# A planned attention and FFN kernel: eight exponentials of block 1 moved into block 0, a column-tiled key projection and another rule for zero matmuls

## The chip, the core and the metric

The kernel runs on one core of a Trainium2 chip. The core has a matrix engine (TensorE, PE in the profile, with its weight loads as PEld), a vector engine (VectorE, DVE), a scalar engine (ScalarE, ACT) for functions such as exp and tanh, a general engine (GpSimd, POOL) and DMA queues, here issued by SyncE (SP). Each engine works through its own list of instructions in order and waits for others by semaphores. Matmuls write to PSUM; everything else lies in SBUF. The metric is the time of one execution on the device, in microseconds; a lower time is better.

## What is computed

One sequence of 2048 tokens of width 512; 32 query heads of width 16 share one key head and one value head; the FFN has width 1792.

```python
x = A_x                                   # 1 x 2048 x 512, bf16
xn = layernorm(x)
q = heads(xn @ wq); k = xn @ wk; v = xn @ wv       # q: 32 heads of 16
s = softmax(q @ k.T * 16 ** -0.5) @ v              # every head, the same k, v
s = join(s) @ wo
g = silu((silu(xn @ w_gate) * (xn @ w_up)) @ w_down)
out = x + s * g
```

## The kernel before

**A plan, then the code.** The kernel holds a small planner in Python (`_Sched`, L182 on). Each piece of work is an `_Op` with an engine, a duration, what it depends on and a function that emits the instructions. The planner runs through time once while the kernel is being built; the order that comes out is then emitted and pinned, engine by engine, with `chain`. On the chip only this order remains: the planner's durations decide who stands behind whom, and waits do the rest.

**Prologue** (`pro_x`, `pro_mm`, `pro_v`). The tokens come in four chunks of 512. For each: statistics, normalization (DVE), transposes by matmul (PE, L434), eviction into `xnT` (DVE, L440), the key projection `pmm` (PE, L443, four steps over the 512 inner elements, with the key weights repeated to all 128 columns in `wk_rep`), its eviction into two key buffers KT[0] and KT[1] (DVE, L447), which are zero in the rows of the other half of the heads, and the value projection (PE, L451). The first chunk also gets the first query tile.

**Attention.** 32 blocks: 16 pairs (a quarter of the tokens and 8 heads), two halves of 4 heads each. A block goes over 16 key tiles of 128 keys, each in two parts x = 0, 1 (2 heads each), so 32 tiles of 128 keys by 2 x 512 queries. Per tile: two score matmuls into one of three PSUM buffers (ring, L836; each uses 32 rows of the array), then the exponential. In ring buffers 0 and 1 this is ACT's work (L887), written to one of eight bf16 buffers `Pb`; in ring buffer 2 it is DVE's (L914, then L927, L930 and L932 for each two tiles). DVE joins once 26 tiles are issued (`D_START`) and the prologue has released its buffers (`d_gate`). When both parts of a key tile have their exponentials, four value matmuls of 32 columns (L719) accumulate into `o_ps`, the one accumulator of the running block. `act_block` gives the block from which ACT takes its next tile: the first one with tiles left. Of block 0, a tile can only be taken once its keys are there (`tile_ready`).

**Fill.** Query projections, the FFN (L470; gate, tanh on ACT at L630, up, down) and the output projection are matmuls in column form: `cmm` cuts the 128 columns of a weight tile into four matmuls of 32 columns each at the four column positions of the array. They are handed out by `pump` at a rate that spreads the FFN over the attention tiles. `g_down` writes the FFN result of 128 tokens into `g2_sb`, which the output stage reads; nothing is in `g2_sb` before.

**PE's choice.** `pe_pick` gives PE's next piece of work at the planner's time F: the next ACT score (time `ts`), the best ready other matmul (`tm`, ranked by `rank`), or a DVE score. If the earliest of them is still at least a matmul (and a mode switch) away, after 26 tiles are issued, and fewer than 7 (`ZN`) column groups were started in the last 3.4 us (`c_log`), a zero group is put in: four column matmuls with zero weights `zw` that add nothing into the open accumulator `o_ps`. In the prologue, `junk` matmuls (L1149) into an unused buffer play that part until DVE's first pair.

Of the kernel before, what the change touches and what calls it, by code (L numbers as in the profile page):

```python
# [33 lines left out]
PB_URG, AHEAD, LAZY, ZN = 6, 16, 8, 7  # L34
# [147 lines left out]
class _Sched:  # L182
# [5 lines left out]
    def __init__(self):  # L188
        self.free = {"PE": 0.0, "ACT": 0.0, "DVE": 0.0, "POOL": 0.0, "DMA": 0.0}
        self.ready = {e: [] for e in self.free}  # L190
        self.done = []
        self.seq = 0
        self.mode = None
        self.key = lambda o: o.prio
# [53 lines left out]
    def place(self, op, start):  # L248
        e = op.eng
        op.start = start  # L250
        if e == "PE":
            op.start += self.switch(op.mode)
            self.mode = op.mode
        op.end = op.start + op.dur
        if e != "DMA":
            self.free[e] = op.end
        self.done.append(op)
        for u in op.users:
            u.left -= 1
            if u.left == 0:  # L260
                self._arm(u)
# [7 lines left out]
def kernel(  # L269
# [13 lines left out]
    nc = tc.nc  # L283
# [75 lines left out]
    Pb = [sb([P, 1024], BF16, f"Pb{i}") for i in range(NPB)]  # L359
    Ub = [sb([P, 2048], U16, f"Ub{i}") for i in range(NU)]  # L360
# [188 lines left out]
    def pro_mm(deps, bk, w, t0, t1, pr):  # L549
        last = None  # L550
        for kc in range(KC):
            last = OP("PE", MMF * (t1 - t0) / 512, deps + [brel[bk], last],
                      lambda kc=kc: e_mm(bank[bk][:, 0:t1 - t0], w, t0, t1, [kc]), (pr, t0), "f", "pmm")
        return last

    def pro_v(c, deps, bk, pr):
        a = None
        for i in range(4):
            a = OP("PE", 0.26, deps + [brel[bk], a, wv_in], lambda i=i: e_vmm(c, i, bank[bk]), (pr, i), "f", "vmm")
        e = OP("DVE", 0.17, [a], lambda: e_vev(c, bank[bk]), (pr - 0.2,), name="vev")  # L560
        brel[bk] = e
        d = [e]
        vs = []
        for i in (-1, 0, 1):
            d = [OP("POOL", 0.33, d, lambda i=i: e_vbuild(c, i), (0,), name="vb")]
            vs.append(d[0])
        v_ready.append(vs)
# [23 lines left out]
    for c in range(1, NSC):  # L591
        evs = pro_x(c, 1.0 + 0.01 * c, ("2a", "2b"), "DVE")
        kp = pro_mm(evs, "m", wk_of, 512 * c, 512 * c + 512, 0.5 + 0.01 * c)
        ka = OP("DVE", 0.62, [kp], lambda c=c: e_kev(512 * c, 512 * c + 512, bank["m"], 0), (0.5, c), name="kev")
        kb = OP("DVE", 0.62, [kp, ka], lambda c=c: e_kev(512 * c, 512 * c + 512, bank["m"], 1), (1.02 + 0.01 * c, c),
                name="kev")
        brel["m"] = kb
        k_ready.append([[ka], [kb]])
        pro_v(c, evs, "2a", 0.7 + 0.01 * c)
# [159 lines left out]
    cur = {"ba": 0, "lastx": 1, "nA": 0, "exp": None, "pair": None, "np": 0, "issued": 0, "lastsc": None, "junk": 0}  # L759
# [4 lines left out]
    pair_blk, c_log = [], []  # L764
# [27 lines left out]
    def act_block():  # L792
        b = cur["ba"]
        while b < NBLK and rem(b, 0) + rem(b, 1) == 0:
            b += 1
        return b if b < NBLK else None

# [60 lines left out]
    def check_done(b):  # L858
        if nx[b][0] == NT and nx[b][1] == NT and not (cur["pair"] is not None and cur["pair"][0] == b):
            assert not unp[b][0] and not unp[b][1]  # L860
            kb_ready[b] = cur["lastsc"]
            finish_block(b)
# [13 lines left out]
    def act_sc(i, b, x, start):  # L876
        sc, t = place_sc(i, b, x, start, MMF)
        cur["lastx"] = x
        cur["ba"] = b
        k = cur["nA"]  # L880
        cur["nA"] += 1
        pi = k % NPB
        pb_rel.append(None)
        if k >= NPB:
            assert pb_rel[k - NPB] is not None
        ex = OP("ACT", 0.904, [sc, pb_rel[k - NPB] if k >= NPB else None, cur["exp"]],
                lambda: nc.scalar.activation(out=Pb[pi][:], in_=ring[i][:], func=ACT.Exp, scale=escale, bias=ebias),  # L887
# [3 lines left out]
        unp[b][x].append((ex, k, t))  # L891
        if unp[b][0] and unp[b][1]:
            half = b % 2
            mms, dps, ks = [], [], []
            for xx in range(2):
                e_, k_, t_ = unp[b][xx].pop(0)
                mms += mm_of(VA, lambda g, k_=k_: Pb[k_ % NPB][:, (g % 2) * 512:(g % 2 + 1) * 512], t_, half,
                             (2 * xx, 2 * xx + 1))
                dps += [e_, v_ready[t_ // 4][0]]
                ks.append(k_)  # L900
            pv = OP("PE", MMF, dps + [oev[b - 1]], pv_emit(b, mms), (1, b, min(ks)), "c", "pv")
            blk_pv[b].append(pv)
            for k_ in ks:
                pb_rel[k_] = pv
# [145 lines left out]

    def pe_pick():
# [3 lines left out]
        b = act_block()  # L1055
# [16 lines left out]
        if ready:  # L1072
# [6 lines left out]
            def rank(o):  # L1079
# [5 lines left out]
                if o.mode == "f":  # L1085
                    return (0.5, o.prio)
# [24 lines left out]
        if junk and T - F > 0.3:  # L1111
            return F, ("junk", None)
        zb = act_block()
        zb = NBLK - 1 if zb is None else zb
        if not junk and cur["issued"] >= D_START and T - F >= MMF + sd.switch("c") \
                and sum(1 for q in c_log[-ZN:] if q > F - 3.4) < ZN:
            for bb in (zb - 1, zb):
                if bb >= 0 and oev[bb].start is None and oev[bb - 1].start is not None \
                        and sd.avail(oev[bb - 1], "PE") <= F and blk_pv[bb] and blk_pv[bb][0].start is not None \
                        and oev[bb].left > 0 and any(o.start is None for o in blk_pv[bb]):  # L1120
                    return F, ("zero", bb)
        if ts is not None and ts <= T + 1e-9:
# [8 lines left out]
    def pe_do(start, what):  # L1131
        kind, arg = what
        if kind == "op":
            sd.run(start, arg)
            if arg.mode == "c":
                c_log.append(start)
            return
        if kind == "zero":
# [5 lines left out]
            c_log.append(start)  # L1144
# [14 lines left out]
        b = act_block()  # L1159
# [136 lines left out]
```

## Time and profile before

| | |
|---|---|
| median of 9 runs | 794.9 us (789.57 to 800.91) |
| the profiled execution | 797.36 us, span 795.5 us |
| mean granted TensorE clock in it | 0.966 |
| busy: PE, DVE, ACT, POOL | 739.8 (93%), 736.7 (93%), 758.5 (95%), 51.2 us (6%) |
| exponentials on ACT (L887) | 778, busy 740.4 us |
| first passes on DVE (L914) | 246, busy 299.4 us |
| score matmuls on PE (L836) | 2048, busy 323.0 us |

The three large engines are all busy for more than nine tenths of the span. A group's busy time counts overlapping stretches once, so it can be less than the count times the mean. The idle time before a group is how long its engine stood still just before it, with the instruction that ended the wait. The clock that TensorE is granted is given as a share of the full one; at 0.5 it runs at half speed.

The prologue in order of time: the first exponential starts at 12.55 us, the first pass of DVE at 48.09 us, the first zero group at 69.3 us.

### The profile page before, as it was taken

How to read it: one execution, taken by the hardware profiler on the slowest of the kernel's cores; microseconds unless marked ns; L12 is line 12 of the kernel's file. 1: busy time of each engine (PE TensorE's matmuls, PEld its weight loads, DVE VectorE, ACT ScalarE, POOL GpSimd, SP SyncE). 2: the span in 40 equal slices, each digit the busy share in tenths (PEclk: the TensorE clock that was granted, in tenths of full speed). 3: DMA queues.
4: the chain of work that ended last, by engine and by line, in shares of the span. 5: the costliest groups of instructions: out<-in, count | busy, mean ns of one | idle time of the engine just before them, and what ended most of it. 6: DMA issues, size and time to landing. Idle time of an engine off the chain costs nothing.

```text
span 795.5 us, 19520 instructions
## 1 busy us (share of the span) xinstructions
PE 739.8 (93%) x8095; PEld 224.0 (28%) x8098; DVE 736.7 (93%) x925; ACT 758.5 (95%) x864; POOL 51.2 (6%) x59
## 2 busy tenths in 40 slices
PE   7899999999999999999999999999999989999994
PEld 3422322222222222222222222222222222222221
DVE  7649999999999999999999999999999989999994
ACT  6679999999999999999999999999999989999993
POOL 2200000100002000000002000000001200000001
PEclk8759999999999999999999999999999989999997
DMA  9300000000000000000001000000000000000001
GB/s 328 111 2 1 13 12 9 15 2 22 2 24 28 18 7 2 23 1 23 3 10 34 9 22 2 23 2 10 15 2 22 29 22 2 2 22 2 24 1 31
DMA packets 19464, 18.50 MB, mean 23 GB/s; under 512 B 8552, under 2 KB 15464, under 8 KB 19368
## 3 DMA queue, kind: packets, MB, share of 16 engines
q1 hardware_dynamic: 17496, 16.37, 6.8%
q8 instruction: 65, 1.06, 0.6%
q10 hardware_dynamic: 1872, 0.82, 0.4%
q14 instruction: 31, 0.25, 0.1%
HBM read 12.62 MB, written 2.34 MB: 19 GB/s over the span
## 4 chain that ended last, share of the span: by engine, by line
PE 51%; ACT 24%; DVE 16%; issue 5%; SPq 1%; DMA 1%; DVEq 0%; ACTq 0%
PE ring L836 22%; ACT Pb L887 19%; PE m_ps L470 17%; PE o_ps L719 10%; DVE Ub L914 6%; ACT th L630 4%; DVE Wb L932 3%; DVE Eb L930 2%; DVE Wb L927 2%; ACT th L647 1%; SPq L746 1%; DVE oa L732 1%; PE ring L434 1%; DVE hT L636 1%; DMA dn<-oa 1%
## 5 line engine op out<-in xcount | busy, mean ns | idle before, releaser
L887 ACT ACTIVATE Pb<-ring 128x1024 bf16<-128x1024 f32 x778 | 740.4, 1221 | 16.8 <-PE ring L836 15.9
L836 PE MATMUL ring<-QB,KT 32*128 32x512 bf16 x2048 | 323.0, 388 | 35.1 <-ACT Pb L887 29.1
L914 DVE TENSOR_SCALAR Ub<-ring 128x1024 uint16<-128x1024 f32 x246 | 299.4, 1217 | 12.4 <-PE ring L836 8.1
L836 PEld LDWEIGHTS <-KT 32*128 32x128 bf16 x2048 | 110.5, 91 | 347.9 <-issue 344.9
L719 PE MATMUL o_ps<-Pb,VA 128*32 128x512 bf16 x1556 | 153.5, 394 | 0.6 <-ACT Pb L887 0.5
L932 DVE TENSOR_TENSOR Wb<-Wb,Ub 128x2048 f16<-128x2048 f16 x123 | 152.0, 1235 | 0.0
L930 DVE TENSOR_SCALAR Eb<-Ub 128x2048 uint16<-128x2048 uint16 x123 | 85.5, 697 | 0.0
L927 DVE TENSOR_SCALAR Wb<-Ub 128x2048 uint16<-128x2048 uint16 x123 | 84.6, 687 | 0.1
L470 PE MATMUL m_ps<-xnT,wg_sb 128*32 128x512 bf16 x896 | 75.5, 389 | 0.7 <-DVE hT L636 0.7
L470 PE MATMUL m_ps<-wd_sb,hT 128*32 128x512 bf16 x896 | 72.2, 384 | 0.2 <-DVE g_sb L649 0.2
L470 PE MATMUL m_ps<-xnT,wu_sb 128*32 128x512 bf16 x896 | 70.6, 388 | 0.2 <-DVE ab L632 0.2
L704 POOL TENSOR_TENSOR oT<-oa,rb 128x512 bf16<-128x512 f32 x15 | 22.1, 1471 | 618.7 <-DMA rb<-dscr 486.9
L719 PEld LDWEIGHTS <-VA 128*32 128x32 bf16 x1556 | 38.9, 94 | 57.8 <-issue 57.4
L719 PE MATMUL o_ps<-Eb,VD 128*32 128x512 f16 x492 | 49.0, 388 | 1.5 <-DVE oa L732 0.6
L719 PE MATMUL o_ps<-Wb,VD 128*32 128x512 f16 x492 | 48.6, 384 | 1.4 <-DVE Wb L932 1.2
L630 ACT ACTIVATE th<-m_ps 128x512 f32<-128x512 f32 x56 | 44.5, 795 | 0.0
L636 DVE TENSOR_TENSOR hT<-ab,m_ps 128x512 bf16<-128x512 f32 x56 | 38.2, 681 | 3.3 <-PE m_ps L470 3.1
L719 PEld LDWEIGHTS <-VD 128*32 128x32 f16 x984 | 28.4, 93 | 41.4 <-issue 40.6
L632 DVE SCALAR_TENSOR_TENSOR ab<-th,m_ps 128x512 f32<-128x512 f32 x56 | 38.2, 682 | 1.9 <-ACT th L630 1.7
L732 DVE COPY oa<-o_ps 128x512 f32<-128x512 f32 (+1 forms) x33 | 22.0, 670 | 6.3 <-PE o_ps L719 5.9
L470 PEld LDWEIGHTS <-wg_sb 128*32 128x32 bf16 x896 | 17.3, 95 | 25.2 <-issue 24.5
L470 PEld LDWEIGHTS <-wu_sb 128*32 128x32 bf16 x896 | 15.4, 95 | 26.4 <-issue 25.2
(102 smaller groups left out, 252.8 us busy)
## 6 DMA issues: line engine op xcount, KB each, us to landing
rb<-dscr SPq DMA_DIRECT2D x15, 256.0 KB
dn<-oa SPq DMA_DIRECT2D x120, 2.0 KB, 1.7
oa<-oa SPq DMA_DIRECT2D x60, 32.0 KB, 2.0
wg_sb<-in_B_w_gate_dram SPq DMA_DIRECT2D x1, 1792.0 KB, 12.5
wu_sb<-in_B_w_up_dram SPq DMA_DIRECT2D x1, 1792.0 KB
wd_sb<-in_B_w_down_dram SPq DMA_DIRECT2D x1, 1792.0 KB, 19.7
out_dram<-xn SPq DMA_DIRECT2D x14, 128.0 KB, 1.9
x_sb<-in_A_x_dram SPq DMA_DIRECT2D x3, 512.0 KB
```

Source lines behind the costliest of these rows:

```text
L470: return [nc.tensor.matmul(out=dst[GRP * j:GRP * j + GRP, :], lhsT=w[:, GRP * j:GRP * j + GRP], rhs=rhs, start=start, stop=stop, tile_posi ...
L630: t_ = OP("ACT", 0.477, [a], lambda: nc.scalar.activation(out=th[i][:], in_=m_ps[:], func=ACT.Tanh, scale=0.5), (0,), name="tanh")
L632: s_ = OP("DVE", 0.6, [t_, ab_rel[i]], lambda: nc.vector.scalar_tensor_tensor(out=ab[i][:], in0=th[i][:], scalar=1.0, in1=m_ps[:], op0=ALU ...
L636: h = OP("DVE", 0.6, [b], lambda: nc.vector.tensor_tensor(out=hT[:, f, :], in0=ab[i][:], in1=m_ps[:], op=ALU.mult), (1,), name="hmul")
L719: r.append(nc.tensor.matmul(out=o_ps[GRP * g:GRP * g + GRP, :], lhsT=lhs, rhs=rhs, start=(n == 0), stop=(n == pv_total[(b, g)] - 1), tile_ ...
L732: oev[b] = sd.new(_Op("DVE", 0.6, [], lambda: [nc.vector.tensor_copy(out=oat[:, a:z], in_=o_ps[:, a:z]) for a, z in cuts], (0.2,), name="o ...
L836: return lambda: [nc.tensor.matmul(out=ring[sl][:, u * 512:(u + 1) * 512], lhsT=KT[half][GRP * g:GRP * g + GRP, t * P:(t + 1) * P], rhs=QB ...
L887: lambda: nc.scalar.activation(out=Pb[pi][:], in_=ring[i][:], func=ACT.Exp, scale=escale, bias=ebias),
L914: lambda: nc.vector.tensor_scalar(out=Ub[ui][:, x * 1024:(x + 1) * 1024], in0=ring[2][:], scalar1=ubias, scalar2=UINF, op0=ALU.add, op1=AL ...
L927: o1 = OP("DVE", 0.6, [pa, pa0, w_rel[u - NE] if u >= NE else None], lambda: nc.vector.tensor_scalar(out=Wb[ei][:], in0=Ub[ui][:], scalar1 ...
L930: o2 = OP("DVE", 0.6, [pa, pa0, e_rel[u - NE] if u >= NE else None], lambda: nc.vector.tensor_scalar(out=Eb[ei][:], in0=Ub[ui][:], scalar1 ...
L932: o3 = OP("DVE", 1.135, [o1, o2], lambda: nc.vector.tensor_tensor(out=Wb[ei][:].bitcast(FP16), in0=Wb[ei][:].bitcast(FP16), in1=Ub[ui][:]. ...
```

## The change

There are three edits, and some bookkeeping.

1. `now_block` takes the place of `act_block` in `pe_pick` and `pe_do`. While block 0 runs, it may return block 1 for ACT's next tile: when block 0's next tile has no keys yet or gets them later than PE is free, and block 1's next tile is ready earlier. Up to 8 such tiles may be taken (`XB`, eight views of 128 x 1024 in `g2_sb`), and a begun pair of parts is completed first. Their exponentials stay in `XB` until block 1 is the running block, since their value matmuls wait for the eviction of block 0 (`oev[b - 1]`).
2. `pro_mm` gets a mode: for chunks 1 to 3 the key projection is emitted by `cmm` (four matmuls of 32 columns per step) instead of one matmul of 128 columns. `pmm` keeps its rank among the prologue's work.
3. Zero groups are decided by `activity(F)`: the sum of planned durations of the PE work started in the last 3.4 us, where a score counts 0.107 and transposes and V projections count nothing. Below 1.7 (`ACTMIN`) a gap is filled; below 1.5 (`ACTLOW`) the gap is measured up to the next ACT score even if a full-array matmul is ready. The condition on 26 issued tiles falls away, and zeros come before `junk`. `fin_b` lets a block that is still being filled take zeros without a value matmul outstanding.

The planned duration of a V projection step goes from 0.26 to 0.13.

```diff
--- before.py
+++ after.py
@@ -31,7 +31,7 @@
 NWARM, NJUNK = 13, 200
 D_START, D_LIM, D_LIM_END = 26, 12, 8
 F_ON, F_OFF = 26, 60
-PB_URG, AHEAD, LAZY, ZN = 6, 16, 8, 7
+PB_URG, AHEAD, LAZY, ACTMIN, ACTLOW = 6, 16, 8, 1.7, 1.5
 TOL, MERGE = 0.12, 0.1
 
 
@@ -255,6 +256,8 @@
         if e != "DMA":
             self.free[e] = op.end
         self.done.append(op)
+        if e == "PE":
+            self.pe_log.append(op)
         for u in op.users:
             u.left -= 1
             if u.left == 0:
@@ -357,6 +360,7 @@
     QB = [sb([P, 512], BF16, f"QB{i}") for i in range(2)]
     NPB, NU, NE = 8, 3, 2
     Pb = [sb([P, 1024], BF16, f"Pb{i}") for i in range(NPB)]
+    XB = [g2_sb[:, 2 * i:2 * i + 2, :].rearrange("p n d -> p (n d)") for i in range(NT // 2)]
     Ub = [sb([P, 2048], U16, f"Ub{i}") for i in range(NU)]
     Eb = [sb([P, 2048], U16, f"Eb{i}") for i in range(NE)]
     Wb = [sb([P, 2048], U16, f"Wb{i}") for i in range(NE)]
@@ -546,17 +550,20 @@
                     evs.append(ev)
         return evs
 
-    def pro_mm(deps, bk, w, t0, t1, pr):
+    def pro_mm(deps, bk, w, t0, t1, pr, mode="f"):
         last = None
         for kc in range(KC):
-            last = OP("PE", MMF * (t1 - t0) / 512, deps + [brel[bk], last],
-                      lambda kc=kc: e_mm(bank[bk][:, 0:t1 - t0], w, t0, t1, [kc]), (pr, t0), "f", "pmm")
+            def emit(kc=kc):
+                if mode == "c":
+                    return cmm(bank[bk][:, 0:t1 - t0], w(kc), xnT[:, kc, t0:t1], kc == 0, kc == KC - 1)
+                return e_mm(bank[bk][:, 0:t1 - t0], w, t0, t1, [kc])
+            last = OP("PE", MMF * (t1 - t0) / 512, deps + [brel[bk], last], emit, (pr, t0), mode, "pmm")
         return last
 
     def pro_v(c, deps, bk, pr):
         a = None
         for i in range(4):
-            a = OP("PE", 0.26, deps + [brel[bk], a, wv_in], lambda i=i: e_vmm(c, i, bank[bk]), (pr, i), "f", "vmm")
+            a = OP("PE", 0.13, deps + [brel[bk], a, wv_in], lambda i=i: e_vmm(c, i, bank[bk]), (pr, i), "f", "vmm")
         e = OP("DVE", 0.17, [a], lambda: e_vev(c, bank[bk]), (pr - 0.2,), name="vev")
         brel[bk] = e
         d = [e]
@@ -590,7 +597,7 @@
     k_ready.append([[ke0, ke1], [kf0, kf1]])
     for c in range(1, NSC):
         evs = pro_x(c, 1.0 + 0.01 * c, ("2a", "2b"), "DVE")
-        kp = pro_mm(evs, "m", wk_of, 512 * c, 512 * c + 512, 0.5 + 0.01 * c)
+        kp = pro_mm(evs, "m", wk_of, 512 * c, 512 * c + 512, 0.5 + 0.01 * c, "c")
         ka = OP("DVE", 0.62, [kp], lambda c=c: e_kev(512 * c, 512 * c + 512, bank["m"], 0), (0.5, c), name="kev")
         kb = OP("DVE", 0.62, [kp, ka], lambda c=c: e_kev(512 * c, 512 * c + 512, bank["m"], 1), (1.02 + 0.01 * c, c),
                 name="kev")
@@ -756,12 +763,12 @@
 
     nx = [[0, 0] for _ in range(NBLK)]
     unp = [[[], []] for _ in range(NBLK)]
-    cur = {"ba": 0, "lastx": 1, "nA": 0, "exp": None, "pair": None, "np": 0, "issued": 0, "lastsc": None, "junk": 0}
+    cur = {"ba": 0, "lastx": 1, "nA": 0, "exp": None, "pair": None, "np": 0, "issued": 0, "lastsc": None, "junk": 0, "nX": 0}
     slot = [None, None, None]
     pb_rel, w_rel, e_rel, wop_rel = [], [], [], []
     open_block(0)
 
-    pair_blk, c_log = [], []
+    pair_blk, fin_b = [], set()
 
     def dve_key(o):
         if o.name in ("dM", "dE", "dW") and pair_blk[o.prio[1]] < cur["ba"]:
@@ -794,6 +801,19 @@
         while b < NBLK and rem(b, 0) + rem(b, 1) == 0:
             b += 1
         return b if b < NBLK else None
+
+    def now_block():
+        b = act_block()
+        if b == 0 and rem(1, 0) + rem(1, 1):
+            r = [tile_ready(bb, act_x(bb)) for bb in (0, 1)]
+            F = sd.free["PE"] + 0.15
+            if unp[1][0] + unp[1][1] and len(unp[1][0]) != len(unp[1][1]) and r[1] is not None and cur["nX"] < len(XB):
+                return 1
+            if len(unp[0][0]) != len(unp[0][1]) and r[0] is not None:
+                return 0
+            if cur["nX"] < len(XB) - 1 and r[1] is not None and (r[0] is None or r[0] > F and r[1] < r[0]):
+                return 1
+        return b
 
     def act_x(b, want=None):
         if want is not None and rem(b, want) > 0 and len(unp[b][want]) < 2:
@@ -858,6 +878,7 @@
     def check_done(b):
         if nx[b][0] == NT and nx[b][1] == NT and not (cur["pair"] is not None and cur["pair"][0] == b):
             assert not unp[b][0] and not unp[b][1]
+            fin_b.add(b)
             kb_ready[b] = cur["lastsc"]
             finish_block(b)
 
@@ -876,32 +897,39 @@
     def act_sc(i, b, x, start):
         sc, t = place_sc(i, b, x, start, MMF)
         cur["lastx"] = x
-        cur["ba"] = b
-        k = cur["nA"]
-        cur["nA"] += 1
-        pi = k % NPB
-        pb_rel.append(None)
+        pre = b == 1 and cur["ba"] == 0 and act_block() == 0
+        if pre:
+            k = -1 - cur["nX"]
+            buf = XB[cur["nX"]]
+            cur["nX"] += 1
+        else:
+            cur["ba"] = b
+            k = cur["nA"]
+            cur["nA"] += 1
+            buf = Pb[k % NPB][:]
+            pb_rel.append(None)
         if k >= NPB:
             assert pb_rel[k - NPB] is not None
         ex = OP("ACT", 0.904, [sc, pb_rel[k - NPB] if k >= NPB else None, cur["exp"]],
-                lambda: nc.scalar.activation(out=Pb[pi][:], in_=ring[i][:], func=ACT.Exp, scale=escale, bias=ebias),
+                lambda: nc.scalar.activation(out=buf, in_=ring[i][:], func=ACT.Exp, scale=escale, bias=ebias),
                 (1,), name="exp")
         cur["exp"] = ex
         slot[i] = ex
-        unp[b][x].append((ex, k, t))
+        unp[b][x].append((ex, k, t, buf))
         if unp[b][0] and unp[b][1]:
             half = b % 2
             mms, dps, ks = [], [], []
             for xx in range(2):
-                e_, k_, t_ = unp[b][xx].pop(0)
-                mms += mm_of(VA, lambda g, k_=k_: Pb[k_ % NPB][:, (g % 2) * 512:(g % 2 + 1) * 512], t_, half,
+                e_, k_, t_, b_ = unp[b][xx].pop(0)
+                mms += mm_of(VA, lambda g, b_=b_: b_[:, (g % 2) * 512:(g % 2 + 1) * 512], t_, half,
                              (2 * xx, 2 * xx + 1))
                 dps += [e_, v_ready[t_ // 4][0]]
                 ks.append(k_)
             pv = OP("PE", MMF, dps + [oev[b - 1]], pv_emit(b, mms), (1, b, min(ks)), "c", "pv")
             blk_pv[b].append(pv)
             for k_ in ks:
-                pb_rel[k_] = pv
+                if k_ >= 0:
+                    pb_rel[k_] = pv
         check_done(b)
         return sc
 
@@ -1048,11 +1076,19 @@
             job["acc"] += w
             fn()
 
+    def activity(F):
+        a = 0.0
+        for o in reversed(sd.pe_log):
+            if o.start < F - 3.4:
+                break
+            a += 0.107 if o.name == "sc" else 0.0 if o.name in ("tr", "vmm") else o.dur
+        return a
+
     def pe_pick():
         F = sd.free["PE"]
         ready = sd.ready["PE"]
         ts = None
-        b = act_block()
+        b = now_block()
         rel = [i for i in (0, 1) if slot[i].start is not None]
         if b is not None and rel:
             i = min(rel, key=lambda i: sd.avail(slot[i], "PE"))
@@ -1082,7 +1118,7 @@
                     if fin or outst >= PB_URG:
                         return (0, o.prio)
                     return (1 if o.name == "dpv" else 3, o.prio)
-                if o.mode == "f":
+                if o.mode == "f" or o.name == "pmm":
                     return (0.5, o.prio)
                 if o.name == "part":
                     return (4, o.prio)
@@ -1108,17 +1144,18 @@
         if not cands:
             return (F, ("junk", None)) if junk else None
         T = min(cands)
-        if junk and T - F > 0.3:
-            return F, ("junk", None)
         zb = act_block()
         zb = NBLK - 1 if zb is None else zb
-        if not junk and cur["issued"] >= D_START and T - F >= MMF + sd.switch("c") \
-                and sum(1 for q in c_log[-ZN:] if q > F - 3.4) < ZN:
+        act_ = activity(F)
+        Tz = ts if act_ < ACTLOW and ts is not None and tm is not None and co.mode == "f" else T
+        if Tz - F >= MMF + sd.switch("c") and act_ < ACTMIN:
             for bb in (zb - 1, zb):
                 if bb >= 0 and oev[bb].start is None and oev[bb - 1].start is not None \
                         and sd.avail(oev[bb - 1], "PE") <= F and blk_pv[bb] and blk_pv[bb][0].start is not None \
-                        and oev[bb].left > 0 and any(o.start is None for o in blk_pv[bb]):
+                        and oev[bb].left > 0 and (bb not in fin_b or any(o.start is None for o in blk_pv[bb])):
                     return F, ("zero", bb)
+        if junk and T - F > 0.3:
+            return F, ("junk", None)
         if ts is not None and ts <= T + 1e-9:
             return ts, ("act", i)
         if tm is not None and tm <= T + 1e-9:
@@ -1132,8 +1169,6 @@
         kind, arg = what
         if kind == "op":
             sd.run(start, arg)
-            if arg.mode == "c":
-                c_log.append(start)
             return
         if kind == "zero":
             o = _Op("PE", MMF, [oev[arg - 1]], pv_emit(arg, [(zw[:], xnT[:, 0, 0:512], g) for g in range(4)]), (0,), "c",
@@ -1141,7 +1176,6 @@
             o.seq = sd.seq
             sd.seq += 1
             sd.place(o, start)
-            c_log.append(start)
             blk_pv[arg].append(o)
             return
         if kind == "junk":
@@ -1156,7 +1190,7 @@
             dve_sc(arg[0], arg[1], start, MMF)
             return
         i = arg
-        b = act_block()
+        b = now_block()
         dt = None
         if d_ok() and slot[2].start is not None and sd.avail(slot[2], "PE") <= start + MERGE:
             x = act_x(b)
```

In the order that results, ACT still has 778 exponentials and DVE 246 first passes. ACT's exponentials 9 to 16 are those of block 1; their sixteen value matmuls stand after ACT's 46th score. There are 25 zero groups instead of 34. Of these, 23 stand between ACT's 4th and its 28th score; before, the first stood after the 46th.

## The prediction

> **What bounds the kernel now.** I read four views, in this order: the slices of the span, the waits of ScalarE (ACT), a table of stretches, and the timeline of the first 66 us.
>
> The page first: slice by slice the granted TensorE clock, and the group that carries ACT.
>
> ```profile
> PEclk8759999999999999999999999999999989999997
> ...
> L887 ACT ACTIVATE Pb<-ring 128x1024 bf16<-128x1024 f32 x778 | 740.4, 1221 | 16.8 <-PE ring L836 15.9
> ```
>
> The clock is below full in the first 60 us (three slices), once near 650 us, and at the end. ACT runs 778 exponentials in 740.4 us, 0.952 us each in net time, and sits idle only 16.8 us before them. Split by time, this idle lies at the start (waits of ACT in 0 to 80 us, then in the rest):
>
> ```profile
> ACT Pb L887 <- PE ring L836: 12.4, 16, 4.9
> ...
> ACT Pb L887 <- PE ring L836: 3.5, 8, 0.9
> ```
>
> The table of stretches (columns: window, its length, busy PE, PEld, DVE, ACT, POOL with counts, clock, DMA share, GB/s):
>
> ```profile
> 15.00:20.00 5.00, 5.00 (x29) 1.67 (x28) 4.07 (x13) 4.82 (x6) 1.43 (x3) 0.50 1.03 398
> 20.00:25.00 5.00, 4.28 (x41) 2.00 (x39) 3.86 (x9) 0.55 (x1) 1.01 (x1) 0.54 1.09 348
> 30.00:35.00 5.00, 4.33 (x39) 1.90 (x40) 4.22 (x12) 5.00 (x6) 2.06 (x4) 0.99 0.00 0
> 40.00:45.00 5.00, 4.70 (x28) 1.20 (x29) 1.41 (x2) 3.77 (x5) 0.00 (x0) 0.50 0.00 0
> 50.00:60.00 10.00, 9.62 (x72) 1.80 (x64) 6.44 (x8) 8.01 (x9) 0.00 (x0) 0.50 0.02 2
> 100.00:200.00 100.00, 96.55 (x1088) 29.39 (x1087) 97.73 (x116) 100.00 (x115) 5.70 (x3) 1.00 0.04 11
> ```
>
> From 80 to 780 us the same table sums to 696.1 us of ACT and 674.7 us of DVE in 700: **ACT is the bound**, idle 3.9 us; DVE has 25.3 us of gaps. So an exponential that starts earlier in the prologue comes off the end, as long as DVE follows. The prologue loses ACT time in two ways: 4.9 us at 20.5 to 25.5, where all 8 tiles of the first 512 keys are done and the next keys do not exist yet, and about 6.5 us in pieces of 0.3 to 0.8 us from 36 to 62 us, where the clock is 0.50, PE is full and each score matmul comes late.
>
> **Prices, from the timeline.** A pair of score matmuls (L836), then a group of four column matmuls (L719), then the next, cold and warm:
>
> ```profile
> 43.84 0.61 PE L836 MATMUL ring<-QB,KT 32*128 32x512 bf16 x2
> ...
> 44.38 0.62 PE L719 MATMUL o_ps<-Pb,VA 128*32 128x512 bf16 x4
> ...
> 33.70 0.39 PE L836 MATMUL ring<-QB,KT 32*128 32x512 bf16 x2
> ...
> 34.02 0.40 PE L719 MATMUL o_ps<-Pb,VA 128*32 128x512 bf16 x4
> ```
>
> Start to start this is 0.54 us cold and 0.32 us warm (0.33 below). A zero group has the form of that L719 group, so it costs the same. Key projection, full array against the column form it gets (both warm):
>
> ```profile
> 30.36 0.61 PE L443 MATMUL m_ps<-xnT,wk_rep 128*128 128x512 bf16 x2
> ...
> 63.00 0.61 PE L470 MATMUL m_ps<-xnT,wg_sb 128*32 128x512 bf16 x8
> ```
>
> Two steps of 512 columns take 0.61 us either way (cold 1.03 and 1.04).
>
> **The change, part by part.** The new instruction order was laid beside the old one; it holds no times. Both orders have 778 ACT tiles and 246 DVE tiles.
>
> 1. *Block-1 tiles into the wait.* After ACT tile 8 the new order puts 8 exponentials of block 1 on the first 512 keys, whose second-half keys (KT of half 1) were written by 14.2 us. They write g2 memory, which g_down fills only after 14 FFN steps; their 16 value matmuls come together at ACT tile 46. So the wait at 20.5 us is filled: keys 512 to 1023 are now needed after tile 16, at 12.55 + 16 x 1.0 = 28.6 us, not after tile 8. What is late next: the transposes of that chunk now stand one by one behind scores 7, 9, 11 and 14 (PE is in order, and a score waits for ACT to free its ring buffer), and its key matmuls stand behind score 16, at about 26.8 us. Then 0.9 us of matmuls, 0.75 us of eviction and 0.4 us of score give the next exponential at about 29.4: some 0.9 us of idle. At the next two chunk ends (tiles 24 and 32), counted the same way, 0.6 and 0.8 us. Left over: 2.3 us, between 1 (DVE writes the keys sooner) and 5 (each chunk end costs what a ring turn costs besides).
>
> 2. *Key projection by column tiles.* 12 matmuls become 48; priced above at no difference. Here a rule speaks against it: the Trainium skill, "TensorEngine Tiling (Array Packing)", says that column tiling turns off the fast weight load and that a change of tiling mode drains the array. The first would add three more weight loads per step: four 32-column loads at 95 ns instead of one at 100 to 150, 12 x 0.25 = 3 us. But the four loads of an L470 group show 0.10 to 0.12 us together in the timeline, since they overlap; I take 0. The drain is inside the 0.33.
>
> 3. *Zero matmuls.* Before: 34 groups, all after ACT tile 46 (first at 69 us), none in the two cold stretches. After: 23 groups between ACT tiles 4 and 28, 2 later. Warm they cost 23 x 0.33 = 7.6 us of PE. I count PE's need from the first score to tile 32: 32 scores and 12 value groups at 0.33, 12 transposes of 4 at 0.35, 12 key steps at 0.25, 12 V groups at 0.2, and the zeros: 31 us warm in the 34 us that ACT takes. They fit, in PE's waits for ACT (cover lost: rival C). Do they hold the clock? The skill's page "TensorE: Matmul & The Clock Gate" (Part 1) has the clock halve after an idle window of some 3.4 us, and return after a busy one. The rows differ: PE is 5.00 of 5.00 busy in 15 to 20 us and the clock is 0.50, so "busy" in the profile is not what counts. By the plain rule the zeros do nothing for a PE that shows no idle, the stretch stays cold, and the sum is rival C's. An estimate from the timeline: give each column group or full matmul its warm 0.215 us, a score pair half of that (it uses half of the rows), transposes and V projections nothing (the same page, Part 4, says transposes do not count as busy). Then the 3.4 us before the fall at 15 us hold about 0.96, before the fall at 35 us 1.06, before the one at 648 us 1.18; the held stretch 28 to 34.5 us has 1.35. The new order gives 1.4 (tiles 8 to 22), 1.5 (22 to 26) and 1.8 (26 to 32) per 3.4 us. Above the falls, by little. I take: the clock holds for most of the prologue. The 31 late zero groups that go free 31 x 0.33 = 10 us of PE, worth nothing while ACT is bound; if one more fall like that at 648 us comes of it, ACT loses 2.9 us (its idle in 645 to 660).
>
> 4. *Split of the work.* The first DVE tile comes after ACT tile 32, near 46.5 us (before: after 28, at 48.1). At ACT tile 59 DVE has 10 tiles behind it instead of 12: two tiles at 2.53 us (299.4 + 152.0 + 85.5 + 84.6 over 246), 5.1 us of DVE work pushed into the part where DVE has gaps of 25.3 us. Cost between 0 and 5.1; I take 1.5, since the gaps are small waits that can only partly close.
>
> **Sum.** ACT idle before L887 in 12 to 62 us was 12.5. 12.5 - 2.3 - 1.5 = 8.7 us less. The profiled execution took 797.36 (span 795.5 and 1.9 around it): 788.7. It lies 2.5 above the median of the nine runs (794.9), from which it would be 786.2; part of that 2.5 is perhaps the fall at 648 us. I take **787 us**.
>
> **Rivals.**
> A (0.62), the forecast: clock full for most of 13 to 47 us. 782 to 790.
>
> B (0.22), the clock falls once for some 20 us. Cold, the PE work counted above is 50 us instead of 31 (scores, values and zeros at 0.54, keys 0.45, transposes 0.5), so a cold microsecond loses 0.38; the slack of 2.8 goes first. 20 x 0.38 - 2.8 = 4.8 us: 788.7 + 4.8 = 793.5, or 791 from the median. For it: the margin of 1.4 against 1.18 is thin. A full give-back to DVE (5.1 instead of 1.5) lands here too, at 792.
>
> C (0.16), slower: **the zeros fill PE and do not buy the clock.** Place: score matmuls in 13 to 47 us, queued behind zero groups of 0.54 us on an in-order PE. It decides from where the extra PE time passes 8.7 + 2.8 = 11.5 us, that is 30 us of cold. Before was cold 36 us (15.2 to 24.6 and 35.4 to 61.9): the same again gives 36 x 0.38 - 11.5 = 2.2 us slower, 799.6; cold throughout (19 us on 31) gives 7 slower. For it: in 46 to 61 us of before PE was full of column groups and still cold. Against: it did return at 62 us from such work.
>
> That the change does nothing is excluded by the order: the block-1 tiles are there, and the 4.9 us wait had no other cause than missing keys.
>
> **How the numbers follow.** 0.5% (4 us) is about what a measurement of this kernel can tell from no change. Faster by more (below 790.9): all of A and a little of B, 0.65. Within: most of B and the mild end of C, 0.20. Slower (above 798.9): 0.15. The range: down to 781 (2.3 and 1.5 at their low ends, less the one fall at 648 us), up to 799 to take in B and the mild end of C. A alone: 782 to 790.
>
> **What would show it.** Right: clock 0.9 or more in the windows from 15 to 45 us; ACT busy above 4.6 of 5 there; ACT's wait on L836's successor in 12 to 62 us 2 to 4 us with no single one above 1.5; first DVE tile at 46 to 47 us. Wrong: clock 0.50 with PE full in those windows (C); or a full clock there with ACT's idle after 80 us well above 4 us (give-back, to DVE's tiles or to new falls where zeros are gone).

## The result and the profile after

The changed kernel takes **786.52 us** in the median of 10 runs (783.4 to 791.69). The kernel before, with the runs taken beside it, stands at 795.96 us (31 runs). The ratio is 0.9889, with a 95% interval of 0.986 to 0.9918: about 9 us less. The profiled execution took 786.9 us, with a span of 785.0 us and a mean granted clock of 0.99 (before: 797.36, 795.5 and 0.966).

The page of the changed kernel: clock by slice, then the group of ACT's exponentials (L914 is the former L887).

```profile
PEclk9999999999999999999999999999999999999998
...
L914 ACT ACTIVATE Pb<-ring 128x1024 bf16<-128x1024 f32 x770 | 728.5, 1168 | 8.1 <-PE ring L856 7.7
```

The clock no longer drops in the first 60 us. 770 exponentials stand in this row; the other 8 write to g2 memory and form a group of their own. The idle time before them fell from 16.8 to 8.1 us. The waits of ACT between 12 and 62 us, where the kernel before had 12.1 us in 15 waits, and then after 80 us:

```profile
ACT Pb L914 <- PE ring L856: 4.1, 4, 1.5
...
ACT Pb L914 <- PE ring L856: 3.6, 9, 0.5
```

The table of stretches, for windows of 5 us (clock third from the end):

```profile
15.00:20.00 5.00, 4.61 (x48) 1.66 (x47) 4.83 (x14) 5.00 (x6) 1.04 (x2) 1.00 1.03 399
20.00:25.00 5.00, 4.73 (x50) 1.89 (x46) 4.54 (x13) 5.00 (x7) 1.01 (x1) 1.00 1.09 348
25.00:30.00 5.00, 4.23 (x68) 2.07 (x69) 4.37 (x11) 3.55 (x5) 1.86 (x4) 1.00 0.24 77
40.00:45.00 5.00, 4.87 (x68) 2.02 (x67) 1.39 (x3) 5.00 (x6) 0.00 (x0) 1.00 0.00 2
```

From 20 to 25 us ACT was busy 0.55 us before and is now busy all 5. The timeline shows what it does there, and what is late next:

```profile
20.24 7.52 ACT L914 ACTIVATE g_sb<-ring 128x1024 bf16<-128x1024 f32 x8
...
29.21 7.44 ACT L914 ACTIVATE Pb<-ring 128x1024 bf16<-128x1024 f32 x8 [1.45 <-PE ring L856]
...
37.65 7.44 ACT L914 ACTIVATE Pb<-ring 128x1024 bf16<-128x1024 f32 x8 [1.01 <-PE ring L856]
...
45.94 1.23 DVE L942 TENSOR_SCALAR Ub<-ring 128x1024 uint16<-128x1024 f32 x1
45.96 4.69 ACT L914 ACTIVATE Pb<-ring 128x1024 bf16<-128x1024 f32 x5 [0.87 <-PE ring L856]
```

The eight block-1 exponentials fill the wait for the second chunk's keys. A shorter wait is left at the end of each chunk: 1.45, 1.01 and 0.87 us. The fourth of the four waits is 0.80 us ahead of the very first exponential.

What the changed kernel still loses is new in place. Two stretches in windows of 2 us:

```profile
192.00:194.00 2.00, 1.53 (x20) 0.33 (x12) 2.00 (x3) 2.00 (x3) 0.00 (x0) 0.74 0.03 3
194.00:196.00 2.00, 2.00 (x16) 0.34 (x12) 1.85 (x3) 1.56 (x2) 0.00 (x0) 0.50 0.01 1
196.00:198.00 2.00, 2.00 (x18) 0.38 (x20) 0.15 (x1) 1.16 (x2) 0.00 (x0) 0.50 0.00 0
```

The clock falls at 193 us for 6.8 us and ACT loses 1.78 us from 190 to 200 us. Another fall comes at 521 us (ACT loses 0.76 us). The profile of before had one late fall, at 648 us. Over the changed kernel's runs the shortest has the highest mean clock and the longest the lowest: 783.4 us at 0.996, 791.69 at 0.985.

### The profile page after: what moved, and what is told of

It reads as the page before. It is cut to its first block, busy times and chain, and to the rows that moved or that the text cites. A ratio compares the mean times of both kernels' runs of the same rounds, so it can differ in the third digit from the quotient of the medians.

```text
span 785.0 us, 19520 instructions
## 1 busy us (share of the span) xinstructions
PE 723.0 (92%) x8097; PEld 219.0 (28%) x8098; DVE 738.4 (94%) x925; ACT 757.1 (96%) x864; POOL 48.4 (6%) x59
## 4 chain that ended last, share of the span: by engine, by line
ACT 38%; PE 33%; DVE 17%; issue 10%; DMA 1%; SPq 1%; POOL 0%; ACTq 0%; DVEq 0%
ACT Pb L914 32%; PE ring L856 14%; PE m_ps L474 11%; PE o_ps L726 7%; DVE Ub L942 6%; ACT th L637 4%; DVE Wb L960 3%; DVE Eb L958 2%; DVE Wb L955 2%; ACT th L654 1%; DVE hT L643 1%; DVE ab L639 1%; DVE oa L739 1%; SPq L753 1%; DMA x_sb<-in_A_x_dram 0%
## 5 line engine op out<-in xcount | busy, mean ns | idle before, releaser
L914 ACT ACTIVATE Pb<-ring 128x1024 bf16<-128x1024 f32 x770 | 728.5, 1168 | 8.1 <-PE ring L856 7.7
L856 PE MATMUL ring<-QB,KT 32*128 32x512 bf16 x2048 | 319.3, 382 | 41.5 <-ACT Pb L914 34.1
L856 PEld LDWEIGHTS <-KT 32*128 32x128 bf16 x2048 | 106.7, 91 | 349.1 <-issue 344.9
L960 DVE TENSOR_TENSOR Wb<-Wb,Ub 128x2048 f16<-128x2048 f16 x123 | 150.8, 1226 | 0.0
L726 PE MATMUL o_ps<-Pb,VA 128*32 128x512 bf16 x1540 | 149.1, 387 | 0.3 <-DVE oa L739 0.2
L955 DVE TENSOR_SCALAR Wb<-Ub 128x2048 uint16<-128x2048 uint16 x123 | 87.2, 710 | 0.3 <-PE o_ps L726 0.2
L711 POOL TENSOR_TENSOR oT<-oa,rb 128x512 bf16<-128x512 f32 x15 | 21.0, 1403 | 605.2 <-DMA rb<-dscr 425.9
L637 ACT ACTIVATE th<-m_ps 128x512 f32<-128x512 f32 x56 | 42.1, 752 | 0.0
```

The source lines that it names most:

```text
L637: t_ = OP("ACT", 0.477, [a], lambda: nc.scalar.activation(out=th[i][:], in_=m_ps[:], func=ACT.Tanh, scale=0.5), (0,), name="tanh")
L726: r.append(nc.tensor.matmul(out=o_ps[GRP * g:GRP * g + GRP, :], lhsT=lhs, rhs=rhs, start=(n == 0), stop=(n == pv_total[(b, g)] - 1), tile_ ...
L856: return lambda: [nc.tensor.matmul(out=ring[sl][:, u * 512:(u + 1) * 512], lhsT=KT[half][GRP * g:GRP * g + GRP, t * P:(t + 1) * P], rhs=QB ...
L914: lambda: nc.scalar.activation(out=buf, in_=ring[i][:], func=ACT.Exp, scale=escale, bias=ebias),
L955: o1 = OP("DVE", 0.6, [pa, pa0, w_rel[u - NE] if u >= NE else None], lambda: nc.vector.tensor_scalar(out=Wb[ei][:], in0=Ub[ui][:], scalar1 ...
L960: o3 = OP("DVE", 1.135, [o1, o2], lambda: nc.vector.tensor_tensor(out=Wb[ei][:].bitcast(FP16), in0=Wb[ei][:].bitcast(FP16), in1=Ub[ui][:]. ...
```

## The experiments

The theory is that the gain has two sources: block-1 tiles fill a wait for keys, and zero matmuls keep enough work in the array that the clock stays full in the prologue. Late falls are then a third matter: the new rule leaves fewer zeros there. The rivals: one of the two parts does everything; PE only has to be busy; the column form counts; late falls are chance that zeros do not touch. Eleven kernels were run in three sets, each beside runs of the kernel before on the same chip. Except where a new plan is mentioned, a variant keeps the planned order and alters only what is emitted, so nothing else moves.

| kernel | median us | ratio to before, 95% interval |
|---|---|---|
| drop_early | 791.39 | 0.9961 (0.9934 to 0.9988) |
| thin_zero | 798.26 | 1.0037 (1.0009 to 1.0065) |
| full_same | 789.65 | 0.9928 (0.9898 to 0.9958) |
| zeros_alone | 796.18 | 1.0007 (0.9979 to 1.0034) |
| after_again | 788.0 | 0.9934 (0.9904 to 0.9964) |
| late_fill_b | 785.49 | 0.9892 (0.9847 to 0.9938) |
| late_fill | 787.45 | 0.9919 (0.9891 to 0.9947) |
| before_drop | 799.35 | 1.0072 (1.0034 to 1.0109) |
| fill_spots | 786.5 | 0.9904 (0.9869 to 0.9938) |
| zeros_filled | 788.65 | 0.9966 (0.9937 to 0.9996) |
| late_fill_b2 | 785.41 | 0.9897 (0.9863 to 0.9932) |

Before stood at 795.27 us beside the first four, 795.38 beside the next four, and 793.34 beside the last three.

### Without the early zeros (drop_early)

```diff
+            zf = (lambda: []) if cur["issued"] < 60 else pv_emit(...)
-            o = _Op("PE", MMF, [oev[arg - 1]], pv_emit(...), (0,), "c", "zero")
+            o = _Op("PE", MMF, [oev[arg - 1]], zf, (0,), "c", "zero")
```

> The changed kernel in its own order, with the 23 zero groups of the prologue left out; the block-1 tiles and the column key projection stay. Theory (the zeros hold the clock, which is worth the pieces of ACT idle after 30 us): the clock falls to 0.50 for 15 us or more in 13 to 62 us, ACT's idle before its exponentials in 12 to 62 us goes from 4.1 to 8 to 11 us, time 790 to 794 us. Rival (the block-1 tiles do it all, zeros idle along): clock still full or fallen without effect, ACT idle about 4 us, time 786 to 788 us. Rival C of the prediction (zeros only cost PE time): faster than the changed kernel by 1 us or more.

Measured: 791.39 us, 4.9 more than the changed kernel's first median, 3.4 more than its second. Both of those come from other sets; beside full_same, the nearest kernel of the same set (789.65 us, described below), it is 1.7 more, and the intervals overlap. So what the early zeros are worth in time lies between 1.7 and 4.9 us and is not known better. Its table of stretches:

```profile
15.00:20.00 5.00, 3.15 (x25) 1.29 (x24) 4.83 (x15) 5.00 (x7) 1.27 (x2) 0.92 1.03 399
20.00:25.00 5.00, 4.35 (x21) 1.23 (x20) 4.72 (x13) 5.00 (x6) 1.01 (x1) 0.50 1.10 347
35.00:40.00 5.00, 4.87 (x42) 1.05 (x42) 0.70 (x3) 4.07 (x5) 0.00 (x0) 0.50 0.01 3
40.00:45.00 5.00, 3.75 (x35) 1.49 (x31) 2.13 (x4) 2.75 (x4) 0.81 (x3) 0.50 0.00 0
```

The clock is at a half again, as before the change, though the block-1 tiles still fill the wait at 20 to 25 us (ACT 5.00). ACT's idle before `Pb` is 11.0 us between 12 and 62 us, the top of what was expected; this profiled execution (796.73 us) was one of the longest of its twelve, so the typical one idles less. Over all profiles the picture is the same: in the nine kernels that emit the full early zeros the clock is full from 12 us to 86 us or longer, in the four that do not (before, before_drop, drop_early, thin_zero) it falls first between 14.4 and 19.2 us. The zeros do hold the clock. Rival C of the prediction, in which they only cost PE time, falls.

### Zeros that keep PE going but send little through the array (thin_zero)

```diff
-   4 x matmul(out=o_ps[32g:32g+32, :], lhsT=zw, rhs=xnT[:, 0, 0:512])
+   8 x matmul(out=o_ps[32g:32g+32, 16r:16r+16], lhsT=zw, rhs=xnT[:, 0, 0:16])
```

> The changed kernel in its own order; each early zero group becomes eight zero matmuls of 16 columns instead of four of 512, so PE has instructions there but little goes through the array. If what holds the clock is the work in the array (the estimate with 0.215 us per column group): as without the early zeros, 790 to 794 us with a clock of 0.50 for 15 us or more before 62 us. If it is enough that PE does something in each wait: as the changed kernel, 786 to 788 us, clock 0.95 or more from 15 to 45 us.

The same windows of thin_zero:

```profile
15.00:20.00 5.00, 4.46 (x72) 2.00 (x70) 4.81 (x14) 5.00 (x6) 1.02 (x1) 0.69 1.02 396
20.00:25.00 5.00, 4.80 (x75) 2.10 (x69) 4.31 (x12) 4.94 (x7) 1.01 (x1) 0.50 1.10 352
40.00:45.00 5.00, 4.12 (x84) 2.22 (x76) 2.33 (x4) 2.64 (x4) 0.82 (x3) 0.50 0.00 0
```

From 15 to 25 us PE is about as busy as in the changed kernel (4.46 and 4.80 us against 4.61 and 4.73), with more matmuls (72 and 75 against 48 and 50). Part of that busy time is longer only because the clock is already low, so the time just before the fall at 16.9 us is the better test. The changed kernel, then thin_zero:

```profile
13.00:17.00 4.00, 3.12 (x29) 1.48 (x28) 3.65 (x11) 4.00 (x5) 1.79 (x4) 1.00 1.03 407
```

```profile
13.00:17.00 4.00, 3.01 (x41) 1.54 (x42) 3.65 (x11) 4.00 (x5) 1.84 (x4) 0.99 1.03 408
```

PE is as busy within 0.11 us, with more matmuls, and here the clock falls. A zero group of thin_zero sends 8 x 16 columns through the array where the changed kernel sends 4 x 512. Busy time and instruction counts do not hold the clock; columns sent through the array do. The direction was as the theory had it, the size was not: 798.26 us lies above the 790 to 794 expected. In the profiles ACT's early idle equals drop_early's (10.9 and 0.5 us against 11.0 and 0.5), and the rest stands later: 7.8 us of idle before `Pb` after 62 us against 5.1, with falls near 525, 605 and 655 us. Why this order met more late falls was not settled.

### The key projection by full matmuls (full_same)

```diff
-                if mode == "c":
-                    return cmm(bank[bk][:, 0:t1 - t0], w(kc), xnT[:, kc, t0:t1], kc == 0, kc == KC - 1)
```

> The changed kernel in its own order, the key projection of chunks 1 to 3 by one matmul of 128 columns per step again. Theory of the prediction (no difference in price): 786 to 787 us, start to start of the key steps 0.22 us as before. Rival (weight loads or mode changes count): key steps differ by 0.1 us or more each, up to 3 us in all, in either direction.

One chunk's four steps in full_same, and the same chunk in the changed kernel:

```profile
26.02 1.04 PE L447 MATMUL m_ps<-xnT,wk_rep 128*128 128x512 bf16 x4
```

```profile
26.31 1.05 PE L474 MATMUL m_ps<-xnT,wk_rep 128*32 128x512 bf16 x16
```

The price is the same to 0.01 us, and ACT's early idle is 4.1 us in both. The median, 789.65 us, looked like a loss of 3 us, but the changed kernel itself, run again in the next set, gave this:

> The changed kernel once more beside the others, to compare on one chip and to be set against full_same (789.65 us). If the column form of the key projection is worth something, 786 to 787 us again; if full_same only met other falls, the two come within 2 us of each other.

788.0 us, 1.65 below full_same, with ratios whose intervals overlap almost wholly (0.9934 and 0.9928). The profile of the full form had one difference: its two late falls came near 594 and 642 us, where ACT lost 2.2 and 3.2 us. Nothing is shown for or against the column form.

### The zeros alone, and the late falls filled (zeros_alone, zeros_filled)

```diff
     def now_block():
         b = act_block()
-        if b == 0 and rem(1, 0) + rem(1, 1):
+        if False:
```

The key projection is in full form here too, and the order is planned anew.

> The zero matmuls by array activity alone: no block-1 tiles, full-array key projection; replanned, again 778 ACT tiles and 246 DVE tiles. Theory (two separate gains): the wait for the second chunk's keys is back, 3.5 to 5 us in one piece near 21 us, the clock holds after it, ACT idle in 12 to 62 us 6 to 8 us, time 789 to 792 us. Rival (the zeros are nearly all of the gain, since a warm prologue makes the keys early): 787 to 788 us. Rival (the block-1 tiles are nearly all): 794 us or more.

At first sight a miss: 796.18 us, no gain at all. But the prologue did what was expected: the clock is 1.00 in every window of 5 us from 15 to 75 us, and ACT's idle between 12 and 62 us is 7.0 us in 5 waits. The time went later. After 80 us ACT waits 12.3 us in 22 waits before `Pb` (the profile of before: 3.5 us), with the clock falling near 85, 145, 265 to 290 and 605 us. So zeros were added to this plan by a rule that touches only gaps which the plan leaves on PE (described with the next set).

> zeros_alone (no block-1 tiles, full-array key projection, 796.18 us) with zero groups added after 60 us by the same rule as late_fill_b. Theory (the block-1 tiles are worth only the wait for keys that is left at full clock, 7.0 against 4.1 us of ACT idle, and the rest of zeros_alone's time was late falls): 788 to 791 us, ACT idle in 12 to 62 us 7 us, after 62 us under 6 us instead of 12.3. Rival (without the block-1 tiles the later plan itself is worse): 793 us or more with few falls.

Measured: 788.65 us. The waits of ACT between 12 and 62 us, and after:

```profile
ACT Pb L914 <- PE ring L856: 7.0, 5, 3.7
...
ACT Pb L914 <- PE ring L856: 2.9, 6, 0.6
```

The early part has not moved, the late part went from 12.3 to 2.9 us, and no window of 10 us before 780 us shows a clock below 1.00. With late falls filled in both, the step from here to late_fill_b beside it (785.41 us, the run late_fill_b2 below) is 3.2 us, against 2.9 us of ACT idle (7.0 to 4.1). The two also differ in the form of the key projection and in the rest of the plan; since the idle time accounts for nearly all of it, I take the 3.2 us as what the block-1 tiles are worth. The longest single wait left, 3.73 us at 20.2 to 24.0 us, is the one they fill; at full clock it is 1.2 us shorter than the 4.9 of before, where the clock was at a half.

### Late zeros (late_fill_b, late_fill, before_drop, fill_spots)

```diff
+    # over the planned PE order, after 60 us, inside an open o_ps accumulation:
+    while o.start - F >= 0.33 and sum(q for s, q in seen if s > F - 3.4) < 1.75:
+        extra[prev] = extra.get(prev, 0) + 1
```

Each entry of `extra` is one more zero group behind that instruction. The weights are those of `activity`.

> The changed kernel in its own order, with 11 more zero groups put after 60 us into planned gaps of PE where the estimate of array activity is under 1.75 in 3.4 us; two each stand near ACT tiles 183 and 519, where the changed kernel's profile shows the clock fall (190 and 520 us). Theory (late falls come from thin stretches that the new rule leaves, and the old rule's 33 late groups had covered them): no fall at these two places, mean clock 0.995 or more, ACT's idle after 62 us some 2.5 us less, time 783 to 785 us. Rival (late falls are a matter of the clock window's phase, zeros there change nothing): 786 to 788 us, falls at the same or other places.

Measured: 785.49 us, and 785.41 us when run again:

> late_fill_b again beside the two others: 784.5 to 787 us if its 785.49 us (six runs) was no accident.

Its profiles show no fall at 190 or 520 us. The first has one at 90 us, the second none before 770 us, with 1.6 us of ACT idle before `Pb` after 62 us (3.6 in the changed kernel). The places at which the changed kernel's profile had fallen got their zeros from the plan alone, and no fall came there; after_again, without these zeros, did not fall there either, so this is in part chance. The medians lie 2.5 us below the changed kernel's on the same chip; the intervals of the ratios overlap, so that late_fill_b beats it is likely and not shown.

> As late_fill_b with a limit of 2.0: 41 more zero groups than the changed kernel. Theory: as late_fill_b or up to 1 us better (782 to 785 us), fewer falls over the runs. Rival (zeros on PE delay scores by their 0.33 us): 787 to 790 us.

With 41 extra groups instead of 11: 787.45 us, where 782 to 785 was expected. More zeros are not better here. Two falls remain in its profile, one of them at 90 us; ACT idle after 62 us is 5.0 us.

> The kernel before in its own order without its 34 zero groups, all of which stand after 69 us. Theory (they held the clock in thin stretches): 2 to 4 falls after 80 us instead of one in the profile, ACT idle there 6 to 12 us instead of 3.5, time 799 to 805 us. Rival (they did nothing): 794 to 797 us, clock after 80 us as before.

The kernel before without its 34 late zero groups: 799.35 us, ratio 1.0072 with an interval that excludes 1. The old zeros were worth 4 us, and the rival that late zeros do nothing falls. Its profiled execution (790.84 us) was the shortest of its twelve and shows three late falls, near 362, 588 and 642 us, where the profile of before has one; ACT's idle before `Pb` after 80 us is 4.6 us, less than the 6 to 12 expected.

Its prologue is that of the kernel before, with no zero taken out, and yet it ran warmer:

```profile
15.00:20.00 5.00, 4.38 (x33) 2.45 (x32) 4.06 (x13) 4.97 (x6) 1.42 (x3) 0.77 1.03 399
20.00:25.00 5.00, 3.65 (x42) 1.68 (x41) 4.67 (x13) 0.46 (x1) 1.50 (x3) 0.89 1.10 347
35.00:40.00 5.00, 4.31 (x38) 1.96 (x39) 2.47 (x4) 4.94 (x6) 0.00 (x0) 1.00 0.01 3
```

Before 62 us the clock is at a half for 13.7 us here and for some 37 us in the profile of before; ACT idles 8.2 us between 12 and 62 us instead of 12.1. How cold the old prologue is differs from one execution to the next, and the prediction had one draw of it.

The fall at 90 us in late_fill_b has a visible start. POOL, DVE and PE in its timeline, then the table in windows of 2 us:

```profile
84.94 1.27 POOL L711 TENSOR_TENSOR oT<-oa,rb 128x512 bf16<-128x512 f32 x1 [38.08 <-DMA rb<-dscr]
...
85.14 1.62 DVE L955 TENSOR_SCALAR Wb<-Ub 128x2048 uint16<-128x2048 uint16 x1
...
87.42 0.40 PE L726 MATMUL o_ps<-Eb,VD 128*32 128x512 f16 x4 [0.55 <-DVE Eb L958]
...
89.75 1.42 PE L474 MATMUL m_ps<-xnT,wu_sb 128*32 128x512 bf16 x12 [0.68 <-DVE ab L639]
```

```profile
88.00:90.00 2.00, 1.12 (x14) 0.47 (x14) 2.00 (x4) 2.00 (x3) 0.00 (x0) 0.96 0.03 8
90.00:92.00 2.00, 2.00 (x18) 0.44 (x14) 1.96 (x2) 0.66 (x2) 0.00 (x0) 0.50 0.00 0
```

The DVE pass L955 takes 1.62 us instead of its median 0.69; it ends 0.55 us after POOL's multiplication, which had begun 0.20 us ahead of it. DVE is then late with `Eb` and `ab`, PE waits 0.55 and 0.68 us that the plan does not know of, and the clock falls. The delay alone is not enough: the first profile of the changed kernel has it too (L955 takes 1.53 us at 84.2 us) and keeps its clock until 193 us. Three more zero groups were put exactly there.

```diff
+    for k, m in ((89, 1), (92, 2)):        # score pairs of the plan, zero groups behind each
+        extra[i] = extra.get(i, 0) + m
```

> late_fill_b with three more zero groups, after its 89th and its 92nd score pair, where its profile shows PE waiting 0.55 and 0.68 us (87 to 89.7 us) just before the clock falls at 90 us. Theory (a fall comes from too little array work in 3.4 us, wherever the gap comes from): no fall at 90 us, ACT's idle after 62 us 1 us or less before its exponentials, 782 to 784.5 us. Rival (the fall there is set by something else): fall stays, 785 to 786 us.

The fall at 90 us is gone:

```profile
88.00:90.00 2.00, 1.83 (x26) 0.59 (x23) 2.00 (x3) 1.73 (x2) 0.00 (x0) 1.00 0.00 0
90.00:92.00 2.00, 2.00 (x28) 0.56 (x30) 2.00 (x4) 1.69 (x2) 0.00 (x0) 1.00 0.00 0
...
126.00:128.00 2.00, 0.89 (x10) 0.37 (x6) 0.60 (x3) 2.00 (x3) 0.00 (x0) 1.00 0.09 19
128.00:130.00 2.00, 1.60 (x14) 0.36 (x17) 2.00 (x4) 0.84 (x2) 0.00 (x0) 0.69 0.20 40
130.00:132.00 2.00, 2.00 (x20) 0.25 (x12) 1.95 (x4) 1.51 (x2) 0.00 (x0) 0.50 0.21 80
```

The time is not better: 786.5 us. Another thin stretch at 126 us, with DVE only 0.60 of 2.00 busy, fell in this execution. No fall came at 90 us, as expected, but one profile cannot tell the filling from chance, and the expected 782 to 784.5 us did not follow.

## Why the prediction was right

The forecast was 787 us in a range of 781 to 799, and 786.52 came. Point by point:

1. **The filled wait.** Right in kind: eight exponentials now stand in it. The wait left over was forecast at 2.3 us (0.9, 0.6 and 0.8) and measured 3.33 (1.45, 1.01 and 0.87), with 0.80 us more ahead of the first exponential, which stood in the 12.5 us and which the sum took away without a reason. The mis-sized term at the first chunk end is ACT's pace: 1.0 us per exponential was taken for reaching the chunk's end at 28.6 us. In a chain eight take 7.44 us, 0.93 each, so ACT was there at 27.76. The keys came as worked out (next exponential forecast for 29.4, measured 29.21). Zeros_filled shows that the block-1 tiles bring 3.2 us: the wait of 4.9 us is only 3.73 us long once the clock is full, so less is to be had by filling it. The prediction's "no other cause than missing keys" left this out: the slow clock was also why the keys were late.
2. **The column form.** No difference, as priced: 1.05 against 1.04 us. The cost of the weight loads that the prediction weighed and took as 0 shows in no time here.
3. **The zeros.** The step with the most doubt held: the clock stayed full in the prologue of all nine profiled kernels that emit the full early zeros. Thin_zero shows that it is work in the array that counts, and drop_early that the clock falls without it. The margin that the prediction gave was partly luck. Counted again with its weights, the stretch that it calls held, 28 to 34.5 us of before, has six score pairs, three value groups and three recorded key matmuls (the trace lacks the fourth): 1.0 to 1.1 per 3.4 us instead of 1.35, and it ends in the fall at 34.9 us. Nor do the late falls keep to one side of a limit: both of the changed kernel's came after 1.18, and other windows of that kernel at 1.18 held. More work in the array makes a fall less likely; no threshold is shown. The count of PE's need also adds up to 31.7 us instead of 31, so its slack was 2.3 us instead of 2.8; with the clock full nothing hung on it.
4. **The split.** The first DVE tile was forecast near 46.5 us and came at 45.94. Of the 1.5 us given back nothing is seen: ACT's idle from 80 to 760 us, by the table of stretches, is 3.9 us before and 4.0 after, with different late falls in the two; DVE is busy 656.8 and 657.7 of 680 us. That gaps absorbed the lag of two tiles fits this, and no run tested it alone.
5. **The sum.** The forecast was 8.7 us less; the profiled spans differ by 10.5. The idle before ACT's exponentials fell by 8.7 (16.8 to 8.1), as forecast to the tenth. That is luck: the wait at the chunk ends was 1.0 us longer, that of the first exponential stayed, the split cost nothing visible, and other late falls came in between. The rest has a term that the sum lacked: ACT's busy time fell by 1.4 us (758.5 to 757.1). That fits a lone exponential taking 1.02 us and one in a chain 0.93, since before the change many in the prologue stood alone; the share of it was not measured. And since the old prologue is cold for a different length in each execution, the 12.5 us that the sum started from were one draw.
6. **The late zeros.** "Worth nothing while ACT is bound" was too short. That the zeros cost nothing there is right; that taking them away costs nothing is not. Before_drop shows 4 us for those of the old plan, and 11 zero groups in thin places of the new one go with a median of 785.49 instead of 788.0 us, a step that is likely and not shown. The prediction had named one more fall as the risk and priced it at 2.9 us; the profiles show 0.76 to 3.2 us of ACT time lost around one.

## What to carry to other kernels

Where a profile shows an engine full and its clock halved, count the work inside the array in each few microseconds, not the busy time: cheap matmuls with many columns in waits that exist anyway can keep the clock full there. While an engine waits for a late input, it can do work of a later stage, if an output buffer is free until then; price the wait at the speed that the rest of the change leaves. When a change replans a whole order, its effect on far stages can hide the local one, as in zeros_alone. To measure one part, keep the order and alter only what is emitted.

## What the hardware showed beyond that

**Thin places fall by chance, on a grid of 3.41 us.** Runs of the changed kernel differ by up to 8.3 us, and its two profiles fell at different places (193 and 521 us; 89 and 635 us). The clock records of the traces show more. Every stretch at half clock between 12 and 770 us, in all thirteen profiles, lasts a whole number of steps of 3.41 us: 3.4, 6.8, 10.2, 17.1, 23.9, 27.3 or 37.5 us (before: 10.2 from 14.4 us, 27.3 from 34.9 us, 6.8 from 649.3 us). The full stretches between them do so as well (after: 187.7 us are 55 steps). Where the grid lies differs: that of after_again is shifted by 0.6 of a step against the first profile. So a thin stretch may lie within one step or across two. That this decides which of them fall is likely, but was not tried.

**POOL and DVE get in each other's way.** DVE's L955 takes 0.69 us in the median and up to 1.63 us (late_fill_b) where POOL's multiplication L711 (1.27 us) had begun first; where DVE's L960 had begun first, the multiplication itself takes up to 2.15 us. The Trainium skill, "SBUF — State Buffer" ("Who interferes with whom"), says that the two share one pair of ports and that whoever issues first has it for the whole instruction while the other waits. The traces agree with a delay of the second one (L955 ends 0.55 us after the multiplication); that the pair is the cause was not tried.
